# Retention in 64-token steps of two batches on 64x64 quarters of the matrix engine, in place of 128-token chunks of one batch

## The chip, the cores and the metric

The kernel runs on one core of one Trainium2 chip. The metric is the device time of one execution in microseconds (us). The engines are called TensorE (matrix products), VectorE, ScalarE and GpSimd; in profile lines they are PE, DVE, ACT and POOL, and PEld is the weight load of TensorE. SP is the queue that issues most transfers.

## The reference

Eight batches of 576 tokens and eight heads of 64 go through retention, which is attention without a softmax and with a decay of gamma^(distance). Its output is the input of a feed-forward layer with a gate of h·cos(h).

```python
# q, k, v: (8 batches, 8 heads, 576 tokens, 64), w_in: (512, 2048), w_out: (2048, 512)
scores = (1 / sqrt(64)) * q @ k^T
gamma  = 1.0 - 2.0 ** (-5.0 - arange(8))                  # one for each head
Dmat   = where(rel >= 0, gamma ** rel, 0.0)               # rel = query position - key position
ret    = (scores * Dmat) @ v
x      = ret, heads side by side                          # (4608 tokens, 512)
h      = x @ w_in
out    = (h * cos(h)) @ w_out                             # float32, (4608, 512)
```

Both kernels use the chunked form. Within a chunk the product of queries and keys is masked to a triangle and multiplied with v ("scores" and "intra"). Earlier chunks come in through a running state of 64x64 for each head, the sum of k^T·v ("state"), which is multiplied with the queries ("inter"). The decay is a factor for each token on v, and another on the queries or on the result.

## The kernel before

There are 40 chunks, five for each batch: four of 128 tokens and one of 64. All work is recorded in one list and split on the engines, with semaphores where one needs another. The parts that the change touches are these.

```python
CH = 128
CHUNKS = [(b, r, min(CH, S - CH * r)) for b in range(B) for r in range(5)]

def load_kv(self, g, i, gate=()):                 # one transfer for a chunk of k or v
    b, r, n = CHUNKS[g]
    slot = g % self.NSTG
    self.P.add("sp", lambda e: e.dma_start(
        ap(self.STG[slot], 2 * DM, 0, n, i * DM, [D, H], [1, D]),
        bass.AP(self.src[1 + i], (b * H * S + CH * r) * D, [[D, n], [S * D, H], [1, D]])),
        r=list(gate), w=[("stg", slot, i)], sem=f"i{slot}_{i}")

# step_s: eight products, 64 rows x 128 columns of the array each (two heads at a time)
e.matmul(ap(self.SC, 1024, 0, n, hp * 512 + c * 128, [1, n]),
         ap(kt, DM, 64 * hp, 64, c * 128, [1, n]), self.queries(g, 64 * hp, 64, c), ...)
#   then VectorE: pt = sc * triangle
# step_st: four products of the full array; two heads each, so half of each result is not wanted
#   then VectorE: sbd = st * block mask
# step_o: "inter", four products of the full array, then "intra", eight of 128 rows x 64 columns
#   then VectorE: xt = bk * decay of the query (table UP)

# ... cut: transposes of k and q by products with the identity, casts on GpSimd ...

# mlp2, end of 128 tokens of the output
self.P.add("sp", lambda e: e.dma_start(
    bass.AP(self.out, (TB * j + 128 * t) * DM + c0, [[DM, 128], [1, cn]]),
    ap(self.OS[o], DM, 0, 128, 0, [1, cn])), r=[("os", o)], sem=f"o{o}")

# schedule, the part around the start of the feed-forward
load_to(8, [("wout", 2)])            # loads of chunks 4 to 7 wait for the third block of w_out
cast_to(6)
self.mlp1(0, 256, 0)                 # the first feed-forward product
self.step_o(3)
# ... cut: the other products of the first 512 tokens; they need no new load ...
run(m[:4], [])
att = [lambda: T(4), lambda: S_(4)] + att_of(4, 7)     # chunk 4 is transposed here, some 20 us later
run(m[4:], att)
```

T(g) transposes the k and q of step g. `att_of` lists T, state, output and scores of each chunk, and `run` spreads them between feed-forward products, which hide what one of them has to wait for.

## Time and profile before

| | before |
|---|---|
| time, median of 2 | 346.68 us (346.17 to 347.19) |
| span of the profiled execution | 347.4 us |
| TensorE busy | 323.8 us, 93% |
| VectorE, ScalarE, GpSimd busy | 189.6, 168.4 and 95.9 us |
| first feed-forward product | 21.35 us |
| last product issued, end of the span | 344.94 and 347.39 us |

The page of the profile for the kernel before comes first. Its second line gives busy time, share of the span and instructions of each engine. The rows of digits are 40 slices of the span, in tenths: busy share of TensorE, clock granted to it, busy share of the DMA engines. The next line gives shares of the chain of waits that ended last. The last ones are issues of transfers, with their count, size, and median time from issue to landing.

```profile
span 347.4 us, 6283 instructions
...
PE 323.8 (93%) x2472; PEld 170.1 (49%) x2512; DVE 189.6 (55%) x304; ACT 168.4 (48%) x276; POOL 95.9 (28%) x137
...
PE   5789779998899999999999999999999999999997
...
PEclk9699989999999999999999999999999999999999
DMA  8899999999228352373546353363920000010012
...
PE 77%; DMA 8%; ACT 4%; DVE 3%; SPq 3%; issue 2%; POOL 2%; DVEq 0%; POOLq 0%
...
out_dram<-os SPq DMA_DIRECT2D x35, 256.0 KB, 2.2
stg<-in_k_dram SPq DMA_DIRECT2D x32, 256.0 KB, 4.3
```

TensorE is the limit: it is nearly always busy and has 77% of the chain. The DMA engines are busy in the first ten slices, which I read as a start bound by transfers. An output store lands 2.2 us after its issue.

The next lines are the timeline of TensorE alone, before, from the first feed-forward product on: start, duration, engine, line, operands and shapes, count, and in brackets idle time ahead of it with what ended it. L380 and L402 are the two layers of the feed-forward, L278 is a transpose of q.

```profile
21.35 0.61 PE L380 MATMUL bk<-xt,win 128*128 128x256 bf16 x4 [0.98 <-DMA win<-in_moe_w_in_dram]
...
22.46 13.63 PE L380 MATMUL bk<-xt,win 128*128 128x256 bf16 x75
35.92 2.75 PE L402 MATMUL bk<-wout,gt 128*128 128x512 bf16 x11
40.21 1.89 PE L402 MATMUL bk<-wout,gt 128*128 128x512 bf16 x8 [1.53 <-DMA wout<-in_moe_w_out_dram]
42.76 0.36 PE L278 MATMUL bk<-idn,qnat 32*128 32x32 bf16 x8 [0.66 <-POOL qnat L221]
...
47.93 0.62 PE L278 MATMUL bk<-idn,qnat 128*128 128x128 bf16 x8 [2.41 <-POOL qnat L221]
```

Between 22 and 40 us TensorE does feed-forward work while the DMA engines bring the weights. The first transpose that needs a late load is at 42.76 us, and it hardly waits. The last of the readings is the view of waits of TensorE, before (total us, times, longest):

```profile
PE bk L278 <- POOL qnat L221: 3.1, 2, 2.4
...
PE bk L380 <- DVE xt L361: 2.3, 5, 0.6
```

TensorE lost only 3.1 us to late casts of q, and 2.3 us to retention results that were not yet there. From the start times of products in this trace: one of 512 columns issues every 216 ns, one of 128 every 56 ns, and a change between full-array and half-array shapes costs about 95 ns more (312 in place of 216).

### The profile page before, as it was taken

To read this page: it belongs to the slowest core of one execution; us is meant where nothing else is said; L and a number is where in the kernel's file an instruction comes from. 1 tells how busy PE (TensorE), PEld (TensorE's weight loads), DVE (VectorE), ACT (ScalarE), POOL (GpSimd) and SP (SyncE) were. 2 spreads that over 40 slices of the span, in tenths; PEclk is the share of its full clock that TensorE was granted. 3 is DMA by queue.
4 is the path that set the end of the run, shared out by engine and by line. 5 is a ranking of instruction groups with operands and counts; after the bars stand their busy time and mean duration, and the time that the engine had idled before them with its cause. 6 is when DMAs were issued, how large, how long until landed. Compare 5 with 4: busy or idle time off the path is not lost.

```text
span 347.4 us, 6283 instructions
## 1 busy us (share of the span) xinstructions
PE 323.8 (93%) x2472; PEld 170.1 (49%) x2512; DVE 189.6 (55%) x304; ACT 168.4 (48%) x276; POOL 95.9 (28%) x137
## 2 busy tenths in 40 slices
PE   5789779998899999999999999999999999999997
PEld 2464335666554545444544544545554544444444
DVE  2697205878756655455646655465656565433300
ACT  7367223667454544555454544545454544444421
POOL 2460267675316131331334131331340000000000
PEclk9699989999999999999999999999999999999999
DMA  8899999999228352373546353363920000010012
GB/s 182 181 187 204 204 230 253 279 210 231 42 72 209 88 138 71 82 172 87 144 110 158 75 148 85 88 164 72 202 77 30 32 30 32 30 62 31 31 62 91
DMA packets 103406, 42.36 MB, mean 122 GB/s; under 512 B 76112, under 2 KB 98896, under 8 KB 103376
## 3 DMA queue, kind: packets, MB, share of 16 engines
q1 hardware_dynamic: 99152, 37.76, 45.2%
q0 software_dynamic: 4224, 4.19, 7.4%
q8 instruction: 20, 0.33, 0.4%
q14 instruction: 10, 0.08, 0.1%
HBM read 36.70 MB, written 9.44 MB: 133 GB/s over the span
## 4 chain that ended last, share of the span: by engine, by line
PE 77%; DMA 8%; ACT 4%; DVE 3%; SPq 3%; issue 2%; POOL 2%; DVEq 0%; POOLq 0%
PE bk L402 33%; PE bk L380 32%; DMA wout<-in_moe_w_out_dram 5%; DMA stg<-in_k_dram 3%; PE sc L302 3%; PE bk L351 2%; SPq L191 2%; PE bk L278 2%; ACT cb L387 2%; DVE gt L390 2%; PE bk L259 2%; PE st L321 2%; PE bk L343 1%; DVE xt L361 1%; POOL win L205 1%
## 5 line engine op out<-in xcount | busy, mean ns | idle before, releaser
L390 DVE TENSOR_TENSOR gt<-bk,cb 128x512 bf16<-128x512 f32 (+3 forms) x164 | 101.8, 625 | 113.2 <-ACT cb L387 99.4
L387 ACT ACTIVATE cb<-bk,cpi 128x512 bf16<-128x512 f32 (+3 forms) x164 | 103.5, 636 | 120.9 <-PE bk L380 120.7
L380 PE MATMUL bk<-xt,win 128*128 128x512 bf16 (+3 forms) x629 | 143.1, 353 | 8.3 <-DVE gt L390 2.5
L402 PE MATMUL bk<-wout,gt 128*128 128x512 bf16 (+1 forms) x580 | 145.1, 376 | 3.4 <-DMA wout<-in_moe_w_out_dram 1.5
L402 PEld LDWEIGHTS bk<-wout,gt 128*128 128x128 bf16 x592 | 55.5, 98 | 64.7 <-issue 3.4
L380 PEld LDWEIGHTS bk<-xt,win 128*128 128x128 bf16 x656 | 56.3, 98 | 54.6 <-DVE xt L361 3.1
L221 POOL CAST nat<-stg 128x512 bf16<-128x512 f32 (+1 forms) x36 | 21.9, 610 | 117.5 <-PE st L321 58.0
L231 POOL TENSOR_TENSOR nat<-stg,wv 128x512 bf16<-128x512 f32 (+1 forms) x40 | 41.7, 1043 | 32.9 <-PE bk L351 19.1
L309 DVE TENSOR_TENSOR pt<-sc,tri 128x1024 bf16<-128x1024 f32 (+1 forms) x40 | 44.2, 1106 | 9.2 <-PE sc L302 9.2
L417 ACT ACTIVATE os<-bk 128x512 f32<-128x512 f32 (+1 forms) x37 | 21.7, 586 | 26.7 <-PE bk L402 26.7
L361 DVE TENSOR_TENSOR xt<-bk,up 128x512 bf16<-128x512 f32 (+1 forms) x40 | 26.7, 668 | 9.2 <-PE bk L351 9.1
L221 POOL CAST qnat<-qstg 128x512 bf16<-128x512 f32 (+1 forms) x44 | 25.8, 612 | 13.5 <-DMA qstg<-in_q_dram 11.7
L219 ACT ACTIVATE kt<-bk 128x512 bf16<-128x512 bf16 (+1 forms) x40 | 22.1, 552 | 12.6 <-PE bk L259 12.6
L219 ACT ACTIVATE qt<-bk 128x1024 bf16<-128x1024 bf16 (+1 forms) x22 | 17.4, 789 | 14.1 <-PE bk L278 14.1
L329 DVE TENSOR_TENSOR sbd<-st,bdm 128x512 bf16<-128x512 f32 x32 | 21.8, 680 | 1.9 <-PE st L321 1.9
L259 PE MATMUL bk<-idn,nat 128*128 128x128 bf16 (+1 forms) x160 | 14.9, 216 | 2.4 <-ACT nat L219 2.4
L278 PE MATMUL bk<-idn,qnat 128*128 128x128 bf16 (+1 forms) x192 | 13.1, 208 | 4.1 <-POOL qnat L221 3.1
L302 PE MATMUL sc<-qt,kt 64*128 64x128 bf16 (+1 forms) x320 | 15.6, 219 | 1.3 <-DVE qt L221 1.2
L302 PEld LDWEIGHTS sc<-qt,kt 64*128 64x128 bf16 (+1 forms) x320 | 9.1, 98 | 15.7 <-issue 13.6
L351 PE MATMUL bk<-pt,nat 128*64 128x128 bf16 (+1 forms) x320 | 16.0, 222 | 0.1
L278 PEld LDWEIGHTS bk<-idn,qnat 128*128 128x128 bf16 (+1 forms) x192 | 10.6, 97 | 10.9 <-POOL qnat L221 4.9
L259 PEld LDWEIGHTS bk<-idn,nat 128*128 128x128 bf16 (+1 forms) x160 | 10.7, 99 | 6.9 <-ACT nat L219 2.9
(36 smaller groups left out, 83.8 us busy)
## 6 DMA issues: line engine op xcount, KB each, us to landing
out_dram<-os SPq DMA_DIRECT2D x35, 256.0 KB, 2.2
stg<-in_k_dram SPq DMA_DIRECT2D x32, 256.0 KB, 4.3
qstg<-in_q_dram SPq DMA_DIRECT2D x16, 512.0 KB, 5.4
stg<-in_v_dram SPq DMA_DIRECT2D x32, 256.0 KB, 5.4
win<-in_moe_w_in_dram POOLq DMA_DIRECT2D x4, 512.0 KB, 8.5
wout<-in_moe_w_out_dram POOLq DMA_DIRECT2D x4, 512.0 KB, 15.2
stg<-in_k_dram SPq DMA_DIRECT2D x8, 128.0 KB, 3.3
qstg<-in_q_dram SPq DMA_DIRECT2D x8, 128.0 KB, 3.2
```

The costliest lines, as they stand in the source:

```text
L219: self.P.add(eng, lambda e: e.activation(dst, src, AF.Copy), r=r, w=w)
L221: self.P.add(eng, lambda e: e.tensor_copy(dst, src), r=r, w=w)
L231: self.P.add(eng, lambda e: e.tensor_tensor(ap(self.NAT[na], 2 * DM, 0, n, DM, [D, H], [1, D]), ap(self.STG[st], 2 * DM, 0, n, DM, [D, H], ...
L259: inst = e.transpose(tb[:, c * 128:c * 128 + n], ap(self.NAT[k], 2 * DM, 0, n, 128 * c, [1, 128]), ap(self.IDN, 128, 0, n, 0, [1, n]))
L278: inst = e.transpose(tb[:, o:o + n], ap(self.QNAT[k], 2 * DM, 0, n, x * DM + 128 * c, [1, 128]), ap(self.IDN, 128, 0, n, 0, [1, n]))
L302: inst = e.matmul(ap(self.SC, 1024, 0, n, hp * 512 + c * 128, [1, n]), ap(kt, DM, 64 * hp, 64, c * 128, [1, n]), self.queries(g, 64 * hp, ...
L309: self.P.add("dve", lambda e: e.tensor_tensor(ap(pt, 1024, 0, n, 0, [128, 8], [h, 2], [1, h]), ap(self.SC, 1024, 0, n, 0, [128, 8], [h, 2] ...
L361: self.P.add("dve", lambda e: e.tensor_tensor(ap(self.XT, 4 * TOK, 0, 128, b * S + CH * r, [TOK, 4], [1, 2], [2, h]), ap(ob, 512, 0, 128, ...
L380: inst = e.matmul(ap(ps, 512, 0, 128, 0, [1, n]), ap(self.WIN, 4 * DFF, 0, 128, c * DFF + 128 * f, [1, 128]), ap(self.XT, 4 * TOK, 0, 128, ...
L387: self.P.add("act", lambda e: e.activation(ap(cb, TB, 0, 128, 0, [1, n]), ap(ps, 512, 0, 128, 0, [1, n]), AF.Sin, bias=self.CPI.ap(), scal ...
L390: self.P.add("dve", lambda e: e.tensor_tensor(ap(gt, NF * TB, 0, 128, f * TB + lo - TB * j, [1, n]), ap(ps, 512, 0, 128, 0, [1, n]), ap(cb ...
L402: return e.matmul(ap(ps, 512, 0, 128, 0, [1, cn]), ap(gt, NF * TB, 0, 128, f * TB + 128 * t, [1, 128]), ap(self.WOUT, NF * DM, 0, 128, f * ...
```

## The change

The intent was to use the array fully. With steps of 64 tokens of two batches, one on partitions 0 to 63 and one on 64 to 127, every retention product is 64x64. Four of them, on the four quarters of the array, can run at once (in the trace after, four start within 10 ns, with a duration of 193 ns each). No product is computed only to be masked away, so the block mask goes. The decay of the queries moves into the casts of q on GpSimd, so the state and the output need no multiplication and ScalarE copies them out. Each of the 36 steps has one `session`: inter of this step with scores of the next, then the rest of those scores, then intra with state in two parts.

The cut diff:

```diff
-CH = 128
-CHUNKS = [(b, r, min(CH, S - CH * r)) for b in range(B) for r in range(5)]
+CH = 64
+NR = S // CH
+NST = (B // 2) * NR
 # load_kv (load_q alike): each load in two, one for each batch
+        for s in range(2):
+            self.P.add("sp", lambda e, s=s: e.dma_start(
+                ap(self.STG[slot], 2 * DM, 64 * s, 64, i * DM, [D, H], [1, D]),
+                bass.AP(self.src[1 + i], ((2 * p + s) * H * S + CH * r) * D, [[D, CH], [S * D, H], [1, D]])),
+                r=list(gate), w=[("stg", slot, i, s)], sem=f"i{slot}_{i}_{s}")
 # ... cut: cast_q becomes a multiplication with the decay table WQ ...
-    # ... cut: step_s, step_st, step_o ...
+    def session(self, g):
+        # ... cut: now, nxt, inter, state, mix() ...
+        def part1(e):
+            return mix(*([self.m_inter(e, g, hp, ob) for hp in range(2)] if inter else []),
+                       *([self.m_scores(e, g + 1, hp, 1 - hp) for hp in range(2)] if nxt else []))
+        def part2(e):
+            return mix(*[self.m_scores(e, g + 1, hp, hp) for hp in range(2)])
+        def part3(e, s):
+            return mix(*[self.m_intra(e, g, s, hp, ob, not inter and s == 0) for hp in range(2)],
+                       *([self.m_state(e, g, 1 - s, hp, s == 0) for hp in range(2)] if state else []))
+        # ... cut: part1 and part2 are issued, VectorE masks the scores ...
+            after = [one] if inter else []
+            for s in range(2):
+                after = [self.P.add("pe", lambda e, s=s: part3(e, s), r=rd, w=wr, after=after)]
+        if state:
+            self.copy("act", self.SBD[g % self.NSB].ap(), self.ST.ap(), ["st"], [("sbd", g % self.NSB)])
+        if now:
+            self.copy("act", ap(self.XT, NST * 512, 0, 128, g * 512, [1, 512]), ob.ap(), [key], [("xt", g)])
 # mlp2, the output store
-        self.P.add("sp", lambda e: e.dma_start(
-            bass.AP(self.out, (TB * j + 128 * t) * DM + c0, [[DM, 128], [1, cn]]),
-            ap(self.OS[o], DM, 0, 128, 0, [1, cn])), r=[("os", o)], sem=f"o{o}")
+        rows = [[1, 2], [2, 32]] if r < 8 else [[1, 64]]
+        for s in range(2):
+            self.P.add("sp", lambda e, s=s: e.dma_start(
+                bass.AP(self.out, ((2 * p + s) * S + CH * r) * DM + c0,
+                        [[a * DM, n] for a, n in rows] + [[1, cn]]),
+                ap(self.OS[o], DM, 64 * s, 64, 0, [1, cn])), r=[("os", o)], sem=f"o{o}_{s}")
 # schedule
         load_to(8, [("wout", 2)])
         cast_to(6)
-        self.mlp1(0, 256, 0)
-        self.step_o(3)
+        self.mlp1(0, 2, 0)
+        T(4)
+        self.session(3)
 # ... cut ...
-        att = [lambda: T(4), lambda: S_(4)] + att_of(4, 7)
+        att = [lambda: T(5)] + att_of(4, 6)
```

`after` makes TensorE wait for its own earlier products. And the rows of a step are held in the order even, odd tokens, so the store's pattern on the side of the output is 2 by 32 rows in place of 128 rows.

## The prediction

> **What bounds it now.** TensorE: the busy table gives it 93% of 347.4 us, and the chain of waits runs through it for 77%. In the matrix-engine timeline a 512-column product issues every 216 ns, so the feed-forward work is about 249 us; the rest is retention, a start bound by DMA (the DMA row: 8 to 9 tenths for 87 us) and small gaps. VectorE (55%) and ScalarE (48%) are not the limit.
>
> **What it takes away.** (a) A 128-token chunk issues four 0.22 us bursts for scores, state, inter and intra (56 ns a product; scores and intra already run in pairs), and enters and leaves a half-array shape twice, at about 95 ns extra each (312 ns instead of 216; 150 instead of 56). [...] After: 20 rounds of up to four quarter products a step, estimated at 32 ns (the cadence of the 64x64 pairs in today's tail chunks), 0.64 us, and two switches. (b) VectorE: masks fall from 1.21 to about 0.68 us, and the 0.68 and 0.73 us block-mask and decay products go; 70 us. ScalarE gains two 0.6 us copies a step, 40 us; GpSimd's q casts go from 0.61 to about 1.04 us. Off the chain.
>
> **What it adds.** (c) TensorE waits for itself twice a session. A 64-column product lasts 193 ns and a consumer starts about 40 ns later: an estimated 0.21 us, and 0.10 where scores fill in, 10 us in all. With (a), retention on TensorE barely shrinks.
> (d) A block's last session stands directly ahead of the first feed-forward product that needs its output, now behind two serial ScalarE copies: an estimated 1.4 us idle at nine boundaries, 12 us (today 0.4).
> (e) The main term. A session also does the next step's scores. The fourth session and step 4's transposes now stand right behind the first feed-forward product, at about 22 us. But step 4's load still waits for the third w_out block, which landed at 37.5 us. TensorE works in order, so it stops until step 4's k and q have landed (about 44 us), been cast (2.1 us), transposed and copied (2.5 us): near 49 us. Today that stretch holds 16 us of feed-forward work and 6 us idle. [...]
>
> **Sum.** Restart 49; then 283 of issue time (feed-forward 249, transposes 13.5, quarters 20.5), 6 switches, 10 self-waits, 12 boundaries, 4 other gaps, [...] 2.7 tail: about 367 us, 80% range 355 to 378. Faster by over 2%: 3%; within 2%: 4%; slower by over 2%: 93%.
>
> **What would show it.** TensorE nearly empty from about 22 to 49 us, released by a GpSimd q cast that itself waits for the q load; clock about half there. Idle before feed-forward products by ScalarE's xt copy at nine block ends. Quarter rounds near 32 ns[...]. VectorE busy near 120 us, ScalarE near 205.
>
> **What would make it wrong.** Loads landing before 44 us; quarter rounds slower (+15 us at 56 ns) or self-waits much cheaper (-7 us); today's gaps around half-array bursts (about 10 us beyond switches, 90 to 305 us) vanishing because everything is pipelined a step ahead.

The recorded sum came to about 367 us. A term of 1 to 2 us for a colder clock is cut from it, with the sentence that it stood on; the terms that are left add up to 366.7 us.

## The result and the profile after

| | before | after |
|---|---|---|
| time, median of 2 | 346.68 us | 391.94 us (391.53 to 392.35) |
| ratio of fast runs, 95% interval | | 1.130 (1.124 to 1.136) |
| span of the profiled execution | 347.4 us | 389.8 us |
| TensorE busy | 323.8 us | 322.7 us |
| VectorE, ScalarE, GpSimd busy | 189.6, 168.4, 95.9 us | 130.3, 199.1, 96.1 us |
| last product issued to end | 2.5 us | 11.3 us |

A ratio is the mean time of one kernel's fast runs over that of the other's of the same rounds, so it is not quite the ratio of the medians quoted beside it.

The kernel got 13% slower. It was outside the predicted range of 355 to 378 us, on the side that had been predicted. The page after, the same parts as above:

```profile
span 389.8 us, 8844 instructions
...
PE 322.7 (83%) x3695; PEld 172.4 (44%) x3728; DVE 130.3 (33%) x233; ACT 199.1 (51%) x331; POOL 96.1 (25%) x120
...
PE   5640089989777999899899989998998999999980
...
PEclk9555559999988999999999999999999999999995
DMA  8999992154469935363434444554321011001112
...
PE 72%; DMA 10%; SPq 6%; ACT 4%; POOL 2%; issue 2%; DVE 0%; DVEq 0%; ACTq 0%; POOLq 0%
...
stg<-in_k_dram SPq DMA_DIRECT2D x72, 128.0 KB, 7.3
...
out_dram<-os SPq DMA_DIRECT2D x70, 128.0 KB
```

Three things stand out. TensorE is nearly empty in the fourth and fifth slices (the two zeros), and its clock reads half speed until well after. It has another dip around slices 11 to 13. And its last slice is a zero. The loads of k are now half as large and take 7.3 us instead of 4.3. The line of the stores has no time to landing: the view counts 16 semaphore events for each transfer, and most of these stores have three (see below). The timeline of TensorE after, at these places:

```profile
24.50 1.04 PE L403 MATMUL bk<-xt,win 128*128 128x256 bf16 x4
48.59 1.03 PE L288 MATMUL bk<-idn,qnat 128*128 128x128 bf16 x8 [23.06 <-POOL qnat L249]
...
51.22 0.26 PE L326 MATMUL bk<-qt,sbd 64*64 64x64 bf16 x2 [1.18 <-ACT kt L228]
...
106.19 0.62 PE L288 MATMUL bk<-idn,qnat 128*128 128x128 bf16 x8 [1.12 <-POOL qnat L249]
...
111.61 0.40 PE L271 MATMUL bk<-idn,nat 128*128 128x128 bf16 x4 [1.61 <-POOL nat L230]
...
118.48 0.84 PE L288 MATMUL bk<-idn,qnat 128*128 128x128 bf16 x8 [2.20 <-POOL qnat L249]
```

The first block is the standstill that had been predicted: one feed-forward product, then 23 us of nothing until a cast of q by GpSimd. The second block had not been predicted. Transposes wait for casts at 106 to 118 us, where 5.9 us were lost in all (5.9 is the time between starts of neighbouring products above their usual cadence, for the change from a first-layer product to a transpose). The waits of TensorE, after:

```profile
PE bk L288 <- POOL qnat L249: 26.4, 3, 23.1
PE bk L403 <- ACT xt L228: 10.3, 9, 1.2
...
PE bk L271 <- POOL nat L230: 1.6, 1, 1.6
```

The second line is the predicted wait at nine block boundaries. What the standstill, the late casts and the end waited for is seen in the chain that ended last, after, in order of time (start, duration, engine and line, count):

```profile
23.52 16.17 DMA wout<-in_moe_w_out_dram
41.70 4.65 DMA qstg<-in_q_dram
46.49 2.05 POOL qnat L249 x2
...
101.86 1.05 SPq L446
104.42 1.17 SPq L199
105.63 2.30 SPq L199
107.97 1.73 SPq L199
111.50 4.75 DMA qstg<-in_q_dram
116.39 2.05 POOL qnat L249 x2
...
364.48 3.64 PE bk L427 x16
369.31 9.15 DMA out_dram<-os
```

The first three lines are the standstill, as predicted: the third block of w_out, which landed at 39.7 us, then a load of q and its cast. Around 102 us the chain goes through the queue that issues transfers: an output store (L446), loads of k and v (L199), then a q load of 4.75 us and its cast. Its last long link is an output store that takes 9.15 us from issue to landing. Before, the chain ends in a stretch of TensorE:

```profile
330.91 9.67 PE bk L402 x44
340.64 4.32 PE bk L402 x35
```

So the output stores became slow, and this was not in the prediction. The trace shows how they differ. The new store's slowest dimension is 2, and each of the 64 such stores has three semaphore events, one about 0.9 us after issue and two later. A store before has 16, the last of the 256 KB ones between 1.8 and 2.0 us after issue. From 384 to 388 us after, with only such stores under way, 13.0% of the 16 DMA engines are busy (view of transfers), which is 2.1 packets at a time; the stores at 343 to 345 us before reach nine tenths of the engines. I read this as two engines for a store of the new pattern. A 128 KB store issued at 318.4 us after landed 5.2 us later, and the last full one, issued at 376.2, only at 388.7 us. My theory was that loads behind such a store wait for these two engines; the experiments test whether the stores delay the loads. The semaphore events of the loads in this trace agree with it: for the k loads issued after 60 us, 14 of the 16 events had come 3.6 us after issue, and the last one only after 8.2 us (medians; 3.2 and 3.4 us in e1_look, the run with other stores below). So the last two events were late (7.4 and 8.2 us) and the others were not. The waits at 106 and 112 us were for such loads; the q load behind the wait at 118 us was itself quick (4.75 us) and had been issued late.

Where the 42.4 us between the two profiles lie can be worked out from the start times of the products. I took 51 us as the cut, which is where TensorE is at full work again after. For each pair of neighbouring products I counted the time up to the usual cadence (216 ns for 512 columns) as issue time of the first, and what is above it as excess.

| from 51 us on | before | after | difference |
|---|---|---|---|
| issue time of feed-forward products still to do | 223.2 | 251.3 | +28.1 |
| issue time of retention products | 26.7 | 21.4 | -5.3 |
| excess inside, into and out of retention | 23.3 | 31.3 | +8.0 |
| all other excess | 6.6 | 9.4 | +2.8 |
| transposes | 13.5 | 13.6 | +0.1 |
| last product to end | 2.5 | 11.3 | +8.8 |
| sum | | | +42.5 |

The first row is what the standstill cost: at 51 us, 28 us more of feed-forward work was still to be done (some 2.7 us of it is a lower clock later on, see e1_look). The second row is what the change was made for.

### The profile page after: what moved, and what is told of

Read it like the earlier page. It is cut to its first block, busy times and chain, and to the rows that moved or that the text cites. A ratio compares the mean times of both kernels' runs of the same rounds, so it can differ in the third digit from the quotient of the medians.

```text
span 389.8 us, 8844 instructions
## 1 busy us (share of the span) xinstructions
PE 322.7 (83%) x3695; PEld 172.4 (44%) x3728; DVE 130.3 (33%) x233; ACT 199.1 (51%) x331; POOL 96.1 (25%) x120
## 4 chain that ended last, share of the span: by engine, by line
PE 72%; DMA 10%; SPq 6%; ACT 4%; POOL 2%; issue 2%; DVE 0%; DVEq 0%; ACTq 0%; POOLq 0%
PE bk L403 31%; PE bk L427 29%; SPq L199 4%; DMA wout<-in_moe_w_out_dram 4%; PE bk L334 4%; PE bk L326 3%; DMA qstg<-in_q_dram 2%; DMA out_dram<-os 2%; PE bk L288 2%; PE bk L271 2%; ACT sbd L228 1%; ACT xt L228 1%; PE sc L308 1%; DMA stg<-in_k_dram 1%; POOL qnat L249 1%
## 5 line engine op out<-in xcount | busy, mean ns | idle before, releaser
L413 DVE TENSOR_TENSOR gt<-bk,cb 128x512 bf16<-128x512 f32 (+1 forms) x164 | 102.2, 627 | 179.8 <-ACT cb L410 175.0
L403 PE MATMUL bk<-xt,win 128*128 128x512 bf16 (+1 forms) x656 | 150.3, 363 | 10.5 <-ACT xt L228 10.3
L410 ACT ACTIVATE cb<-bk,cpi 128x512 bf16<-128x512 f32 (+1 forms) x164 | 103.0, 637 | 79.6 <-PE bk L403 79.5
L427 PE MATMUL bk<-wout,gt 128*128 128x512 bf16 (+1 forms) x561 | 137.3, 373 | 2.4 <-ACT os L441 0.7
L427 PEld LDWEIGHTS bk<-wout,gt 128*128 128x128 bf16 x592 | 57.4, 98 | 66.9 <-ACT os L441 2.1
L239 POOL TENSOR_TENSOR nat<-stg,wv 128x512 bf16<-128x512 f32 x36 | 37.5, 1042 | 13.0 <-DMA stg<-in_v_dram 12.7
L376 DVE TENSOR_TENSOR pt<-sc,tri 128x512 bf16<-128x512 f32 x36 | 24.6, 683 | 46.0 <-PE sc L308 46.0
L288 PE MATMUL bk<-idn,qnat 128*128 128x128 bf16 x144 | 12.5, 233 | 29.2 <-POOL qnat L249 26.4
L249 POOL TENSOR_TENSOR qnat<-qstg,wq 128x512 bf16<-128x512 f32 x32 | 32.8, 1041 | 11.4 <-DMA qstg<-in_q_dram 11.4
L228 ACT ACTIVATE kt<-bk 128x512 bf16<-128x512 bf16 x36 | 21.4, 594 | 12.0 <-PE bk L271 12.0
L334 PE MATMUL bk<-pt,nat 64*64 64x64 bf16 x576 | 23.6, 204 | 3.2 <-PE st L316 0.5
L228 ACT ACTIVATE xt<-bk 128x512 bf16<-128x512 f32 x36 | 21.4, 594 | 2.3 <-PE bk L334 2.3
L308 PE MATMUL sc<-qt,kt 64*64 64x64 bf16 x576 | 20.6, 204 | 1.5 <-DVE qt L230 0.8
L316 PE MATMUL st<-nat 64*64 64x64 bf16 x512 | 21.1, 205 | 0.0
L334 PEld LDWEIGHTS bk<-pt,nat 64*64 64x64 bf16 x576 | 15.5, 113 | 8.6 <-PE st L316 6.4
L326 PEld LDWEIGHTS bk<-qt,sbd 64*64 64x64 bf16 x512 | 11.4, 115 | 15.5 <-ACT cb L410 10.3
```

Of the source, the lines that this page charges most:

```text
L228: self.P.add(eng, lambda e: e.activation(dst, src, AF.Copy), r=r, w=w)
L239: self.P.add(eng, lambda e: e.tensor_tensor(ap(self.NAT[na], 2 * DM, 0, 128, DM, [D, H], [1, D]), ap(self.STG[st], 2 * DM, 0, 128, DM, [D, ...
L249: self.P.add(eng, lambda e, x=x, step=step: e.tensor_tensor(ap(self.QNAT[k], 2 * DM, 0, 128, x * DM, [D, H], [1, D]), ap(self.QSTG[k], 2 * ...
L288: inst = e.transpose(tb[:, o:o + 128], ap(self.QNAT[k], 2 * DM, 0, 128, x * DM + 128 * c, [1, 128]), self.IDN.ap())
L308: yield lambda c=c: e.matmul(ap(self.SC, 1024, 64 * s, 64, hp * 512 + c * 64, [1, 64]), ap(kt, DM, 64 * hp, 64, c * 128 + 64 * s, [1, 64]) ...
L326: yield lambda c=c, s=s: e.matmul(ap(ob, 512, 64 * hp, 64, c * 128 + 64 * s, [1, 64]), ap(sbd, 512, 64 * hp, 64, s * 256 + c * 64, [1, 64] ...
```

## The experiments

There were 12 runs. Before them I held theory A: the part that the prediction lacked is the shape of the output stores, which slows them and, through the common queue, the loads. Where the expectations speak of two engines, this is the reading of the trace given above (2.1 packets at a time from 384 to 388 us; two of 16 events late, 8.2 us in place of 3.6). Its rival is that nothing new happened and that the costs that were in the prediction (the standstill, the waits of TensorE for itself, the copies by ScalarE at the boundaries) are all larger than estimated. The texts of what was expected are as they were recorded, but for two cuts in e6_quads that are marked.

### e1_out32: stores with a slowest dimension of 32

```diff
-        rows = [[1, 2], [2, 32]] if r < 8 else [[1, 64]]
         for s in range(2):
-            self.P.add("sp", lambda e, s=s: e.dma_start(
-                bass.AP(self.out, ((2 * p + s) * S + CH * r) * DM + c0,
-                        [[a * DM, n] for a, n in rows] + [[1, cn]]),
-                ap(self.OS[o], DM, 64 * s, 64, 0, [1, cn])), r=[("os", o)], sem=f"o{o}_{s}")
+            for x in range(2 if r < 8 else 1):
+                n, step = (32, 2) if r < 8 else (64, 1)
+                self.P.add("sp", lambda e, s=s, x=x, n=n, step=step: e.dma_start(
+                    bass.AP(self.out, ((2 * p + s) * S + CH * r + x) * DM + c0, [[step * DM, n], [1, cn]]),
+                    ap(self.OS[o], DM, 64 * s + 32 * x, n, 0, [1, cn])), r=[("os", o)], sem=f"o{o}_{s}_{x}")
```

> The changed kernel (392 us); only its output stores differ: each 64-row half goes out as two stores of 32 rows each, so that the slowest dimension of the pattern is 32 instead of 2. Theory A (a pattern whose slowest dimension is 2 is carried by two of the sixteen DMA engines; the stores queue up on those two, and loads behind them wait): the time after the last matmul falls from 11.3 us to 3 to 4, the TensorE waits for casts of late loads between 99 and 131 us (about 5.4 us) mostly go, total 376 to 382. Rival B (halving the DMAs costs issue time, 0.64 us each on the issuing queue; the shape does not matter): more stores make it the same or worse, 390 to 396, tail 11 us or more.

Measured: 377.6 us, ratio to the kernel before 1.086 (1.080 to 1.092), against 391.9 and 1.130 for the change as it was made. The same bytes in twice as many stores are 14 us faster. Theory A holds for this part.

### b1_out2: the kernel before, with two-row stores

```diff
-            bass.AP(self.out, (TB * j + 128 * t) * DM + c0, [[DM, 128], [1, cn]]),
+            bass.AP(self.out, (TB * j + 128 * t) * DM + c0, [[DM, 2], [2 * DM, 64], [1, cn]]),
```

This puts the rows in a wrong order (relative error 1.40). It gives the kernel before the shape of the store and nothing else.

> The kernel before (346.7 us); only the row order of the output stores differs, so that their slowest dimension is 2 (rows within a tile land permuted: wrong on purpose). Theory A (two DMA engines carry them): stores land 9 to 11 us after issue instead of 2.0; the tail after the last matmul grows from 2.4 to 10 us or more, loads behind stores land late too, total 354 to 362. Rival B (the number of stores matters, not the shape; it is unchanged here): 346 to 348.

Measured: 367.0 us against 348.2 for the kernel before, ratio 1.056 (1.052 to 1.061). The direction is as theory A has it, and the size is beyond what I had expected (354 to 362). Its issues of transfers, and the waits of its TensorE:

```profile
stg<-in_k_dram SPq DMA_DIRECT2D x32, 256.0 KB, 8.2
qstg<-in_q_dram SPq DMA_DIRECT2D x16, 512.0 KB, 9.0
```

```profile
PE bk L278 <- POOL qnat L221: 7.0, 2, 6.1
```

The stores alone double the time of a k load, 8.2 us in place of 4.3, and TensorE waits 6.1 us for a cast of q at 87 us. The time from last product to end grows from 2.5 to 14.8 us. These are both of the effects seen in the changed kernel, and there is no 64x64 product in this one. The rival theory has no place for it.

### e2_late4: the standstill taken away

```diff
-        T(4)
-        self.session(3)
+        self.session(3, nxt=False)             # without the scores of step 4
 # ... and later, after four parts of the second layer:
-        att = [lambda: T(5)] + att_of(4, 6)
+        att = [lambda: T(4), lambda: self.session(3, now=False), lambda: T(5)] + att_of(4, 6)
```

> The changed kernel; only the order differs: the fourth session no longer computes the scores of step 4, and these and step 4's transposes come after the first four units of the second product, where the kernel before has them. Theory A (TensorE stands still from 25 to 51 us only because these instructions wait in order for loads gated on a weight load; worth 26 us less some 6 us that return when the loads are still late at 45 us): 370 to 375. Rival (the start is bound by DMA whatever the order, so the wait just moves): over 386.

Measured: 376.9 us, ratio 1.086 (1.080 to 1.092). This is 15 us less, 2 us short of the predicted 370 to 375. The 23 us wait is gone, but the view of waits for this kernel shows what took its place:

```profile
PE bk L288 <- POOL qnat L249: 15.4, 5, 5.9
```

The longest of these, 5.9 us, is at 78 us, and another of 2.8 is at 93 us. A kernel that gets there earlier asks for its loads earlier, and with slow stores ahead of them they are not there. So a part of the gain was turned into a new wait.

### e3_xtfirst: the copy of the output ahead of that of the state

```diff
+        if now:
+            self.copy("act", ap(self.XT, NST * 512, 0, 128, g * 512, [1, 512]), ob.ap(), [key], [("xt", g)])
         if state:
             self.copy("act", self.SBD[g % self.NSB].ap(), self.ST.ap(), ["st"], [("sbd", g % self.NSB)])
-        if now:
-            self.copy("act", ap(self.XT, NST * 512, 0, 128, g * 512, [1, 512]), ob.ap(), [key], [("xt", g)])
```

> The changed kernel; only the two ScalarE copies at the end of a session are swapped, so that the output of the session is copied before the state. Theory: at the nine block boundaries TensorE waits 1.2 us for two copies in a row, so each boundary with a state copy loses 0.6 us: 4 to 5 us less, 387 to 388. Rival (another wait ends last there, such as the activations queued on ScalarE): under 2 us.

Measured: 388.8 us (385.3 to 390.9), 3 us less in the medians, between the 4 to 5 that were expected and the rival's under 2; the runs spread over more than this difference. In the profile, the excess at the changes from retention to the first layer falls from 14.0 to 10.1 us, so 3.9 us less. The order of the two copies is a part of the boundary wait, as had been thought, and not all of it.

### b2_early4: the kernel before, with the standstill

```diff
         self.mlp1(0, 256, 0)
+        T(4)
+        S_(4)
         self.step_o(3)
 # ...
-        att = [lambda: T(4), lambda: S_(4)] + att_of(4, 7)
+        att = att_of(4, 7)
```

> The kernel before, only with the transposes and scores of its chunk 4 moved up behind the first feed-forward product, as the change orders them. Theory (in-order stop on loads gated by a weight load, whatever the chunk shape): TensorE idle from 22 to about 45 us, and part of the 6 us lost later there comes back: 362 to 368. Rival (the change's stop is owed to its own loads or casts): within 5 us of 347.

Measured: 365.4 us against 347.5, ratio 1.051 (1.047 to 1.055), within the expected 362 to 368. TensorE stands still for 20.68 us, until 42.19 us, with a cast of q as the releaser, as its next products in order wait for it. Nothing but the place of one chunk's transposes and scores in the order of TensorE costs 18 us here. The step of the prediction about the standstill is shown.

### b3_out64: the kernel before, with each store in two halves

```diff
-            bass.AP(self.out, (TB * j + 128 * t) * DM + c0, [[DM, 128], [1, cn]]),
-            ap(self.OS[o], DM, 0, 128, 0, [1, cn])), r=[("os", o)], sem=f"o{o}")
+                bass.AP(self.out, (TB * j + 128 * t + 64 * s) * DM + c0, [[DM, 64], [1, cn]]),
+                ap(self.OS[o], DM, 64 * s, 64, 0, [1, cn])), r=[("os", o)], sem=f"o{o}_{s}")   # for s in 0, 1
```

> The kernel before, only with each output store cut into two of 64 rows in natural order, as many stores as the change has but each on a dimension of 64. Theory A (shape): within 1.5 us of the kernel before, stores land 2 us after issue. Rival B (number of stores): 5 us or more slower.

Measured: 349.96 us against 347.52, ratio 1.007 (1.002 to 1.011). This is a little more than the 1.5 us expected, and still only an eighth of what the two-row pattern costs. A half lands 2.4 us after issue. It is the pattern that makes the stores slow, and not their number.

### e4_out32_late4: both repairs

The edits of e1_out32 and e2_late4 together.

> The changed kernel with both repairs: stores of 32 rows, and step 4's transposes and scores moved late. If stores on two engines and the in-order stop are the two causes of the unforeseen and foreseen loss, and the late loads that grew to 16 us of waits in the run with the move alone were behind such stores, the gains add to more than their sum (14 and 15): 355 to 361, tail 3 to 4 us, waits for casts of late loads under 8 us. Rival (both repairs free the same time): 368 to 376.

Measured: 357.1 us, ratio 1.025 (1.021 to 1.030), within the expected 355 to 361. One by one the repairs gave 14 and 15 us. Together they give 35, because the wait that e2_late4 got in place of the standstill was one for loads, which the stores no longer delay: casts of q by GpSimd now hold TensorE for 2.3 us, not 15.4.

### e5_all: and the sessions earlier

e4_out32_late4 with the copies in the order of e3_xtfirst, and every retention part three feed-forward parts earlier:

```diff
-                while k < n * (i + 1) // m:
+                while k < min(n, n * (i + 4) // m):
```

> As the run before, and in addition the output copy ahead of the state copy and every session emitted three feed-forward units earlier, so that no block boundary waits for it. Theory: the nine waits of 1.2 us (10 us in all) go: 345 to 351, level with the kernel before. Then what is left of the change is about zero on TensorE: fewer shape switches and issue time against the self-waits. Rival (sessions were also early enough before; another wait comes up in their place): 353 or more.

Measured: 350.95 us, ratio 1.009 (1.005 to 1.012), at the upper end of the expected 345 to 351. The line of waits of the first layer for ScalarE's copy, 10.3 us in nine waits, is gone from the view. The boundary waits are shown to be a matter of order and not of ScalarE's speed.

### e6_quads: the quarters in an order that needs one wait fewer

In the changed kernel, half of the intra products add to results of inter that came from the other half of the array's rows, and `after` makes TensorE wait until inter has ended. That this wait is needed was my assumption; no run leaves it out with that order. Not every pair of products on different rows waits: the two inter products of a pair, on rows 0 to 63 and 64 to 127 of the array, start 3 to 4 ns apart in the changed kernel and write the same columns of one PSUM tile on different partitions (0 to 63 and 64 to 127), and the output was correct in each of the runs e1 to e7. Here intra follows inter on the same quarter, and the second half of the scores comes between the two halves of intra:

```diff
-            return mix(*[self.m_intra(e, g, s, hp, ob, not inter and s == 0) for hp in range(2)],
-                       *([self.m_state(e, g, 1 - s, hp, s == 0) for hp in range(2)] if state else []))
+            return mix(*[self.m_intra(e, g, s ^ hp, hp, ob, not inter and s == 0) for hp in range(2)],
+                       *([self.m_state(e, g, 1 - (s ^ hp), hp, s == 0) for hp in range(2)] if state else []))
 # order: part1, part3(0) with no wait, part2, part3(1) with `after` on part3(0)
```

> As the run with both repairs and early sessions (351 us), but inside a session the quarters are handed out so that the intra products follow the inter products on the same row and column quarter, state takes the other two, and the scores' second half stands between the two halves of intra and state. The first self-wait of a session then has nothing to guard and goes [...], the second is covered in part by four rounds of scores. Theory (the two self-waits cost 12 us in that run's trace: 9.3 before the second half, 2.9 before the first): 5 to 8 us less, 343 to 346. Rival [...]: under 2 us less.

Measured, five rounds: 345.74 us against 347.81 for the kernel before, ratio 0.996 (0.992 to 0.999). It is 5.2 us under e5_all, as expected (4.5 by the two ratios), and its output is correct, with one of the two waits replaced by keeping dependent products on the same quarter. The excess between state or scores and intra falls from 10.5 us in e5_all to 4.7. The timeline of TensorE at one session of this kernel (L326 inter, L334 intra, L308 scores, L427 second layer):

```profile
108.97 0.22 PE L326 MATMUL bk<-qt,sbd 64*64 64x64 bf16 x2
...
109.31 0.23 PE L334 MATMUL bk<-pt,nat 64*64 64x64 bf16 x4
109.38 0.29 PE L308 MATMUL sc<-qt,kt 64*64 64x64 bf16 x8
...
109.89 1.04 PE L427 MATMUL bk<-wout,gt 128*128 128x512 bf16 x4
```

The whole session takes 0.92 us, from 108.97 to 109.89. That is the first version that is not slower than the kernel before, by 0.4%, which is within the 2% that counts as the same.

### e7_start: a faster start

e6_quads with loads issued ahead of the constants, half of the first two steps' loads issued by ScalarE's queue, more of the dummy products of `warm` at the start, and the next four steps spread over the second layer:

```diff
-            self.P.add("sp", lambda e, s=s: e.dma_start(
+            self.P.add("act" if s and g < 2 else "sp", lambda e, s=s: e.dma_start(       # load_kv; load_q alike
...
+            warm(2)
             self.session(g - 1)
             if g < 3:
-                warm(2)
+                warm(4)
...
-        run(m[4:], att)
+        run(m[4:9], [])
+        T(4)
+        run(m[9:11], [])
+        self.session(3, now=False)
+        # ... cut: T(5), session(4), T(6), session(5) in the same way
```

> As the run beside it, and the start mended: half of the first two steps' loads issued by ScalarE's queue, more warm-up products, and step 4 and 5's work spread over the first second-product tiles. Theory (the start of the change is late because twenty half loads cost 0.64 us of issue each, against a 2.3 us earlier weight load before, and because TensorE's clock stays at half until 30 us): first feed-forward product at 22 us instead of 24.3, granted clock near 1.0 between 20 and 30 us, total 3 to 6 us less than the run beside it, 338 to 342, below the kernel before (347). Rival (the start is bound by DMA throughput alone): within 1.5 us of the run beside it.

Measured, five rounds: 345.59 us, ratio 0.994 (0.990 to 0.997). I had expected 338 to 342, and there is no clear gain over e6_quads, as the rival had it (within 1.5 us).

### e1_look: the profile of e1_out32 in an undisturbed run

The same kernel as e1_out32.

> The changed kernel with stores of 32 rows once more, for a profile in the fast state (the first fell in a slow one). Theory A: stores land about 2 us after issue, 3 to 4 us from the last matmul to the end, waits of TensorE for casts of late loads (products to transposes) under 1 us instead of 5.9, span 375 to 378. Rival B: stores as late as before the repair.

Measured: 375.3 us, a single run, so its state is unknown; its clock (0.94) and its time agree with the fast runs of e1_out32. Its page, issues of transfers:

```profile
stg<-in_k_dram SPq DMA_DIRECT2D x72, 128.0 KB, 3.5
...
out_dram<-os SPq DMA_DIRECT2D x132, 64.0 KB, 1.7
```

and the waits of its TensorE:

```profile
PE bk L288 <- POOL qnat L249: 22.6, 1, 22.6
PE bk L403 <- ACT xt L228: 10.3, 9, 1.2
```

The k loads are the same transfers as in the changed kernel, and they land after 3.5 us and not 7.3. The late waits for casts are gone: of 26.4 us in three waits, the one of the standstill is left. The end comes 3.4 us after the last product, and not 11.3. The spans differ by 16.2 us: 7.9 at the end, 5.4 in excess and 2.7 in issue time after 51 us (the clock no longer falls to 0.77 between 110 and 120 us), and 0.8 in a standstill that ends earlier. That adds up to 16.8, with an error of about half a us from the cut.

### e7_look: the profile of e7_start

The same kernel as e7_start.

> The kernel with the mended start once more, for a profile in the fast state. If the mended start did nothing because DMA throughput sets it: first feed-forward product still within 1 us of 24.4 and the third w_out block still at about 40 us, although the loads were issued earlier. If it did something that was lost later: first product at 22 to 23 us with a granted clock near 1.0 from 20 to 30 us, and the wait for step 4's casts near 49 us longer by as much.

Measured: 346.1 us, a single run, state unknown. Its first feed-forward product is at 22.86 us (24.43 in e6_quads), and its clock is 1.00 between 20 and 30 us (0.52 there). So the mended start did do something, and it was lost later. But the third block of w_out landed only 0.8 us earlier, at 39.2 us, and the wait for step 4's casts near 49 us was shorter than in e6_quads (1.24 us and 3.04), not longer as I had expected. This line of its timeline of TensorE has one of the new waits:

```profile
66.86 0.61 PE L293 MATMUL bk<-idn,qnat 128*128 128x128 bf16 x4 [2.98 <-POOL qnat L254]
```

Another, of 4.10 us, is at 85 us. In all, TensorE waits 8.6 us for casts of q by GpSimd, in four waits, against 4.4 us in two in e6_quads. The q load behind the wait at 67 us was issued at 60.8 us, and at 58.2 us in e6_quads; the one behind the wait at 85 us at 77.7 us, and at 74.2 us there. This run places the transposes of steps 4 to 6 later, so eight stores and not four go out just ahead of the first of these loads, and in both kernels the issuing queue has no pause from 40 to 80 us (some 0.65 us for a half load, 0.5 us for a store). So what TensorE gained at the start was lost again to waits for loads. Whether bytes, the number of issues or their order in this queue holds the loads back is not shown: the run changed the start and the order at once.

## Why the prediction was right or wrong

- **That it gets slower, and the standstill: right.** The prediction had TensorE nearly empty from about 22 to 49 us. It was empty from 25.5 to 48.6 us and at full work at 51.2. The clock was 0.50 from 10 to 52 us in the windows of the profile; the half rate began before the standstill, in the thinly filled start, and lasted through it (in e6_quads, without a standstill, it was 1.00 between 30 and 40 us). b2_early4 shows the cause alone, on the kernel before: +18 us. The 2.2 us by which the restart came later than predicted are those of the start itself: the third block of w_out landed at 39.7 us and not at 37.5. The 20 half loads of the first steps took the issuing queue until 15.4 us, some 0.65 us each, where the ten loads before were out by 12.7 us. That this is the reason is argued and not shown: in e7_look five of the twenty went out on ScalarE's queue, and the last one still left only at 14.8 us.
- **Quarter rounds of four products in 32 ns: right.** Where all four quarters are in use, four products start within 10 ns, and the next four 32 ns after the first (the changed kernel, at 150 us). Retention products have 21.4 us of issue time after 51 us, and 26.7 before. The estimate for all of the issue time was 283 us. It was 286.3, and 283.6 in e1_look, so most of what is over belongs to the stores.
- **Waits of TensorE for itself, 10 us: right.** They were 8.3 us from state to intra and 2.8 from scores to intra, at 29 places each after 51 us, about 0.24 and 0.10 us a time where the prediction had 0.21 and 0.10. e6_quads took more than half of it away.
- **Boundaries, 12 us: right but for a little.** The view of waits has 10.3 us in nine waits. e5_all shows them to go away with an earlier place.
- **VectorE near 120 and ScalarE near 205, off the chain: right.** They were 130 and 199 us.
- **The sum was wrong in its last terms, "4 other gaps" and "2.7 tail".** They are about those of the kernel before, which holds only if the output stores and the loads behind them stay as quick as they were; the list of what the change adds doesn't name the stores at all. The tail measured 11.3 us. The other gaps held 5.9 us of transposes that waited for loads behind the stores. The two together, with a lower clock after those waits (0.77 from 110 to 120 us), are the 16.2 us of span between the changed kernel and e1_look, and 14 us of time in e1_out32. With the stores mended the time is 377.6 us, which is inside the predicted range, at its upper end.

The prediction's terms add up to 368 us with the cut term for the clock, taken as 1.5. The measured ones are 51.2 + 286.3 + 40.7 (all excess, for which the prediction had 33.5: its switches, self-waits, boundaries, gaps and the cut clock term) + 11.3 = 389.5, against a span of 389.8. The 21 us between the sums are 8.6 in the tail, 7.2 in the excess, 3.3 in issue time and 2.2 in the restart.

What the change was for has a clear answer too. Issue time and excess of retention after 51 us come to 50.0 us before, 52.7 after, 39.6 in e5_all and 32.5 in e6_quads (one profile each, that of e6_quads being its fastest execution). So the quarters, with early sessions and the order of e6_quads, take up to 17 us less of TensorE's time. The kernel before was not given earlier retention parts, so how much of this it could have without quarters is untested; its own waits for retention results are 2.3 us. Little of the 17 us shows in the time, because e6_quads has 232.2 us of feed-forward work left at 51 us where the kernel before has 223.2, and its transposes wait more. In e7_look a start that TensorE got through sooner gained nothing in the end. What stays open is whether fewer bytes or fewer issues at the start would let the 17 us through; no run with the 64-token steps had fewer of either.

## What to carry to other kernels

When a change permutes the rows that a tile holds, look at the store (or load) at the other end: its access pattern gets a new slowest dimension, and the time of the transfer, and of those queued behind it, can double although the bytes are the same (b1_out2, with a slowest dimension of 2 in place of 128: a k load of 256 KB took 8.2 us in place of 4.3, and the end after the last product 14.8 us in place of 2.5). Work out a prediction from every line of the diff, each transfer with it, before any term is carried over from the old profile. And of two faults repaired one at a time, each may show only part of its gain, as the wait moves to the other one: repair both before judging the idea.
